# Half products for a third expert in the last three pairs, and for the fourth in the last pair

## The chip, the cores and the metric

The kernel runs on one core of a Trainium2 chip. The metric is the device time of one execution in microseconds, the median of several runs. The engines named below are TensorE (PE, with its weight loads shown apart as PEld), ScalarE (ACT), VectorE (DVE), GpSimd (POOL) and SyncE (SP, which issues DMAs). Each has a queue of its own; they meet through semaphores.

## The reference

Two stages follow each other. The first is attention over 4 batches, 8 heads, 768 positions and 64 values per head: heads 0, 2 and 6 see all earlier positions, the other five only the first 4 positions and a window of 64. Its output, laid out as 3072 tokens of 512 values, is the input x of the second stage, a mixture of 4 experts that are all evaluated for every token:

```python
N, D, E, F = (3072, 512, 4, 1024)
p = domain_probs / (domain_probs.sum(-1, keepdims=True) + 1e-09)
for e in range(E):
    h = np.maximum(x @ w1[e], 0.0)
    out += p[:, e:e + 1] * (h @ w2[e])
```

Since p is positive, it may be multiplied into x before the Relu; the kernel does so in the stretch that matters here.

## The kernel before

**Tiles and pairs.** The 3072 tokens are 24 tiles of 128. The first four tiles are done one way, while attention still supplies inputs. The other twenty are ten pairs of two tiles (256 tokens), in `pair_steps`. The change touches the last three of these pairs: the eighth (tiles 18 and 19), the ninth (20 and 21) and the tenth (22 and 23). By then attention is over; its buffers for keys (`kSf`), values (`vSf`, `kR`) and its PSUM banks `pV` are free for other use.

**Layer 1, plain.** `plain_layer1(e)` computes h = Relu(x w1) of one expert for 256 tokens. It is a generator with four steps. A step issues 8 matmuls of 256 columns (line 1199) into a PSUM bank from a pool of four (`pA`), then one Relu by ScalarE (line 1208).

**Layer 1 by half products.** `winograd_layer1(e, x, y)` computes the same with 7 products of half-size blocks instead of 8 (the scheme of Strassen in Winograd's form). It is a generator with seven steps. A step issues 8 matmuls of 128 columns (line 1228). Products 1, 3, 5 and 7 accumulate in bank x, 4 and 6 in bank y, product 2 goes to a bank of its own. ScalarE copies the partial sum out of the bank after products 1, 3 and 4 (line 1238). VectorE adds such a copy to a bank after products 2, 5 and 6 and applies the Relu (line 1245). ScalarE applies the Relu to bank x after product 7 (line 1278). A product may write a bank only after its last reader is done. The scheme needs sums of inputs (`scaled_sums`, lines 1166 and 992: three VectorE instructions, and one more after product 4) and sums of the weights (`first_weight_sums`, line 992: three into buffers, and a fourth that overwrites a block of w1), which are made once per expert.

**Which experts.** All pairs use half products for expert 3 (`EW[0]`). The last three (`two`) use them for expert 2 too (`EW[1]`), and the last two (`three`) for expert 1 (`EW3`), each with banks x and y: experts 3 and 1 share the two `pO` banks, expert 2 then has the two `pV` banks. Expert 0 is always plain.

**Order.** An order of steps is written out by hand for each kind of pair: a list of rows with the generators to advance and an operation to issue after them. `a`, `b` and `third` are the half products of experts 3, 2 and 1, and `n` a plain step. In the eighth pair it is (one step of `a`, `b` or `n` at a time): a a n a a n a a n n a b n b b n b b n b n b. In the ninth and tenth it is a b seven times, n, and then third third n three times, and third. So each engine's queue holds its work in exactly this order.

**Layer 2.** The same scheme is applied to h w2, over all four experts at once: 7 products of 16 matmuls of 256 columns (line 1361) in the two `pO` banks. The sums of blocks of h that it needs are made by VectorE: `first_sum` (line 1174) at the end of layer 1, second, third and fourth sums (line 992) during layer 2. During layer 2 VectorE also scales the next pair's inputs by the probabilities (`scale_inputs`, line 1150), which SP loads (`load_probs`, line 1127), and its outputs are stored by SP. Adds of layer 2 are on line 1384. The last pair ends with two shorter products (line 1453).

Of the kernel before, what the change touches and what calls it, by code (L numbers as in the profile page):

```python
# [19 lines left out]
def kernel(  # L20
# [42 lines left out]
    DMP = DM // P  # L63
# [50 lines left out]
    EW = (E - 1, E - 2)  # L114
    KH, FN = DMP // 2, F // 2
# [7 lines left out]
    kSf = pers.tile([P, NT * NSH * P], FP16, name="kS")  # L123
    vSf = pers.tile([P, NT * NSH * P], FP16, name="vS")
# [881 lines left out]
    t1 = {(EW[0], n): t1sb[:, n, :, :] for n in range(3)}  # L1006

    def first_weight_sums(e):

        return [  # L1010
            lambda: minus(t1[e, 0], w1_part(e, 0, 1), w1_part(e, 0, 0)),
            lambda: minus(t1[e, 1], w1_part(e, 1, 1), t1[e, 0]),
            lambda: minus(t1[e, 2], w1_part(e, 1, 0), t1[e, 1]),
            lambda: minus(w1_part(e, 0, 1), w1_part(e, 1, 1), w1_part(e, 0, 1)),
        ]
# [11 lines left out]
    EW3 = E - 3  # L1027

    def room_for_third():

        n = KH * FN
        for i in range(3):
            t1[EW3, i] = vSf[:, i * n : (i + 1) * n].rearrange("p (c f) -> p c f", c=KH)

    def inputs_for_third():
        n0 = 3 * KH * FN
        x = vSf[:, n0 : n0 + DMP * PC]
        own_room[EW3] = x.rearrange("p (c x) -> p c x", c=DMP)
# [72 lines left out]
    PC = PT * P  # L1111
# [10 lines left out]
    xs_of = [None]  # L1122

    def load_probs(nt0):
        pB_of[nt0] = moe.tile([P, PT, E, P], FP32, name="pB", tag="pB", bufs=1)
        rows = p_rows[nt0 : nt0 + PT, :]
        nc.sync.dma_start(
            out=pB_of[nt0].rearrange("p t e x -> p (t e x)"),
            in_=bass.AP(rows.tensor, rows.offset, [[0, P], [1, PT * E * P]]),
        )  # L1130
# [26 lines left out]
    second_set = set()  # L1157
# [6 lines left out]
    def scaled_sums(e):  # L1164

        nc.vector.tensor_tensor(
            out=x_sum(e, 0), in0=x_part(e, 1, 0), in1=x_part(e, 1, 1), op=ALU.add
        )
        minus(x_sum(e, 1), x_sum(e, 0), x_part(e, 0, 0))
        minus(x_part(e, 1, 0), x_part(e, 0, 0), x_part(e, 1, 0))  # L1170

    def first_sum(e, n=1):
        k = slice(e * HT, (e + n) * HT)
        nc.vector.tensor_tensor(
            out=S1[:, k, :], in0=A21[:, k, :], in1=A22[:, k, :], op=ALU.add
        )
# [9 lines left out]
        return nt0 >= pairs[-LAST]  # L1186

    def three(nt0):
        return nt0 >= pairs[-2]

    def pair_steps(nt0, nxt):

# [28 lines left out]
        def winograd_layer1(e, x, y, kept=kept):  # L1221

            ns = HT * KH * mm_ns(P)

            def product(ps, w, a, first):
                for f in range(HT):
                    for ct in range(KH):
                        nc.tensor.matmul(  # L1228
                            out=ps[:, f * P : (f + 1) * P],
                            lhsT=w_tile(e, w[:, ct, :], f),  # L1230
                            rhs=a[:, ct, :],
                            start=(first and f == 0 and ct == 0),
                            stop=(ct == KH - 1),
                            skip_group_check=True,
                        )

            def keep(n, ps):
                nc.scalar.copy(out=kept[n], in_=ps)  # L1238

            def block(n):  # L1240
                return blocks[:, n, e * HT : (e + 1) * HT, :]

            def add(n, ps, b):

                nc.vector._custom_dve(  # L1245
                    TENSOR_ADD_SAT,
                    out=block(b),
                    in0=ps.rearrange("p (f x) -> p f x", f=HT),
                    in1=kept[n].rearrange("p (f x) -> p f x", f=HT),
                    s0=LARGEST,  # L1250
                    s1=0.0,
                )

            def t(n):
                return t1[e, n]

            product(x, w1_part(e, 0, 0), x_part(e, 0, 0), True)
            keep(0, x)
            yield ns, 0.5
            z = bank()  # L1260
            product(z, w1_part(e, 1, 0), x_part(e, 0, 1), True)
            add(0, z, 0)
            yield ns, 0.5
            product(x, t(1), x_sum(e, 1), False)
            keep(1, x)
            yield ns, 0.5
            product(y, t(0), x_sum(e, 0), True)
            keep(2, y)
            minus(x_part(e, 0, 1), x_part(e, 0, 1), x_sum(e, 1))
            yield ns, 0.5  # L1270
            product(x, w1_part(e, 0, 1), x_part(e, 1, 0), False)
            add(2, x, 3)
            yield ns, 0.5
            product(y, w1_part(e, 1, 1), x_part(e, 0, 1), False)
            add(1, y, 2)
            yield ns, 0.5
            product(x, t(2), x_part(e, 1, 1), False)
            nc.scalar.activation(
                out=block(1), in_=x.rearrange("p (f x) -> p f x", f=HT), func=AF.Relu
            )  # L1280
            yield ns, 0.5
# [3 lines left out]
        a, b = (winograd_layer1(e, *y) for e, y in zip(EW, (banks, banks[::-1])))  # L1285
        if three(nt0):

            second_set.add(EW[1])
            more_kept = kSf[:, 0 : 4 * HT * P].bitcast(FP32)
            more_kept = [more_kept[:, n * HT * P : (n + 1) * HT * P] for n in (0, 1, 0)]  # L1290
            more_banks = [pV.tile([P, DM], FP32, name="pV", bufs=2) for _ in range(2)]
            b = winograd_layer1(EW[1], *more_banks, more_kept)
            third = winograd_layer1(EW3, *banks)

        more, last_more = [], None
        if nt0 == pairs[-LAST - 2]:
            room_for_more_sums()
            more = first_weight_sums(EW[1])
        elif nt0 == pairs[-LAST - 1]:
            last_more = first_weight_sums(EW[1])[3]  # L1300
        elif nt0 == pairs[-3]:
            room_for_third()
            more = first_weight_sums(EW3)
            last_more = more[3]
        if not two(nt0):
            n = itertools.chain(*(plain_layer1(e) for e in range(E - 1)))
            order = (
                ((n,), lambda: scale_inputs(nt0, 1)),
                ((n,), more[0] if more else None),
                ((n, a), lambda: last_weight_sum(E - 1) if nt0 == pair0 else None),  # L1310
                ((n, a), None),
                ((n, a), lambda: scale_inputs(nt0, 2)),
                ((n, a), lambda: load_probs(nxt)),
                ((n, a), more[1] if more else None),
                ((n, a), more[2] if more else None),
                ((n, a), lambda: first_sum(0, 2)),
                ((n,), None),
                ((n, n), lambda: first_sum(2, 2)),
                ((), lambda: scale_inputs(nxt, 1) if two(nxt) else None),
            )  # L1320
        elif three(nt0):
            n = plain_layer1(0)
            order = (
                ((), lambda: scaled_sums(EW[1])),
                ((a, b, a, b), lambda: load_probs(nxt) if nxt else None),
                ((a, b, a, b), None),
                ((a, b, a, b), None),
                ((a, b), lambda: scaled_sums(EW3)),
                ((n,), None),
                ((third, third, n), lambda: first_sum(EW[0])),  # L1330
                ((third, third, n), lambda: first_sum(EW[1])),
                ((third, third, n), lambda: first_sum(0)),
                ((third,), lambda: first_sum(EW3)),
            )
        else:
            n = itertools.chain(plain_layer1(0), plain_layer1(1))
            order = (
                ((a, a, n), more[0] if more else None),
                ((a, a, n), lambda: load_probs(nxt) if nxt else None),
                ((a, a, n), more[1] if more else None),  # L1340
                ((n,), lambda: scaled_sums(EW[1])),
                ((a, b, n), more[2] if more else None),
                ((b, b, n), lambda: first_sum(0)),
                ((b, b, n), lambda: first_sum(EW[0])),
                ((b, n, b), lambda: (first_sum(1), first_sum(EW[1]))),
            )
        for steps, op in order:
            for x in steps:
# [7 lines left out]
        x = pO.tile([P, DM], FP32, name="pO", bufs=2)[:, 0:HN]  # L1356
        y = pO.tile([P, DM], FP32, name="pO", bufs=2)[:, 0:HN]
# [47 lines left out]

        last = nxt is None
        ahead = nxt and two(nxt)
        if ahead and three(nxt):
            inputs_for_third()
        half = KT // 2 * mm_ns(HN), PSHARE  # L1410
        yield from product(x, A11, b(0, 0), True)
# [62 lines left out]
    pairs = list(range(pair0, NTILE, PT))  # L1474
# [145 lines left out]
```

The softmax here doesn't subtract the row's maximum and nothing guards it: scores larger than these inputs give would overflow.

## Time and profile before

| | us |
|---|---|
| median of 3 runs (lowest, highest) | 376.77 (376.42, 377.32) |
| the profiled execution | 376.68 |
| its span in the profile | 375.0 |
| TensorE busy in the span | 367.9 |
| layer 1 of the eighth pair | 13.24 (from 296.10 to 309.34) |
| layer 1 of the ninth pair | 12.88 (from 321.56 to 334.44) |
| layer 1 of the tenth pair | 13.01 (from 346.66 to 359.67) |

Times inside the profile are microseconds from the start of the span. In the timelines a row is one instruction, or several that follow each other: start, duration, engine, line, operation, the written tensor and what it is read from, shape and count. In brackets stands how long the engine had been idle and what ended that. The end of a matmul is modelled from its start, so the distance of two starts says how long the first occupied TensorE; a reader that waits for it can start only after the modelled end.

### The profile page before, as it was taken

What the parts mean: (1) busy time and instruction counts of PE and PEld (TensorE: products, weight loads), DVE (VectorE), ACT (ScalarE), POOL (GpSimd) and SP (SyncE); (2) the same over time, 40 slices, a digit from 0 to 9 for tenths busy, and PEclk for the clock granted to TensorE, in tenths of its full rate; (3) what the DMA queues carried; (4) which work ended last, traced back from release to release, by engine and by line L of the source; (5) the groups of instructions that cost most, each with busy time, mean ns of one, the idle gap of its engine ahead of it and who ended that gap; (6) DMA issues with size and microseconds to landing.
All of it is one profiled execution on the core that took longest, in us unless ns stands there. A gap on an engine that the chain in (4) does not pass through costs nothing.

```text
span 375.0 us, 10225 instructions
## 1 busy us (share of the span) xinstructions
PE 367.9 (98%) x4176; PEld 311.1 (83%) x4176; DVE 279.0 (74%) x599; ACT 227.4 (61%) x475; POOL 113.3 (30%) x155
## 2 busy tenths in 40 slices
PE   8899999999999999999999999999999999999996
PEld 5755466668998988999989898998899998998996
DVE  7774768697788669868658858957767968969762
ACT  3863478547785785765676955784778362450630
POOL 8924673982058038115601650320000000000000
PEclk9999999999999999999999999999999999999999
DMA  8999999999699569977904990951220300300101
GB/s 161 155 204 208 195 189 192 186 207 100 97 109 149 101 94 116 163 112 56 207 14 60 171 159 14 133 127 14 67 73 3 98 18 0 114 2 2 58 3 56
DMA packets 123747, 39.24 MB, mean 105 GB/s; under 512 B 113728, under 2 KB 116356, under 8 KB 123700
## 3 DMA queue, kind: packets, MB, share of 16 engines
q0 software_dynamic: 85824, 19.01, 58.7%
q1 hardware_dynamic: 36276, 19.18, 21.8%
q8 instruction: 32, 0.52, 0.6%
q10 hardware_dynamic: 1600, 0.39, 0.5%
q14 instruction: 15, 0.12, 0.1%
HBM read 44.89 MB, written 6.34 MB: 137 GB/s over the span
## 4 chain that ended last, share of the span: by engine, by line
PE 95%; DVE 2%; ACT 2%; issue 0%; ACTq 0%
PE pO L1361 31%; PE pA L1199 23%; PE pO L1228 9%; PE pA L1065 7%; PE pO L1086 7%; PE pA L678 5%; PE pV L734 2%; PE pV L806 2%; PE pA L1228 2%; PE pV L1228 1%; PE pO L448 1%; PE pA L576 1%; ACT es L696 1%; DVE xs L1150 1%; PE pA L1453 0%; ACT rc L824 0%
## 5 line engine op out<-in xcount | busy, mean ns | idle before, releaser
L1361 PEld LDWEIGHTS <-hA 128*128 128x128 f16 x1104 | 104.9, 98 | 12.3
L1199 PE MATMUL pA<-xs,w1sb 128*128 128x256 f16 x800 | 101.3, 273 | 0.0
L1199 PEld LDWEIGHTS <-w1sb 128*128 128x128 f16 x800 | 74.7, 98 | 7.9
L1208 ACT ACTIVATE hA<-pA 128x512 f16<-128x512 f32 x100 | 59.6, 598 | 31.2 <-PE pA L1199 29.0
L1361 PE MATMUL pO<-w2sb,hA 128*128 128x256 f16 x640 | 76.7, 272 | 0.0
L696 ACT ACTIVATE es<-pA 128x384 f16<-128x384 f32 (+2 forms) x122 | 59.2, 511 | 26.9 <-PE pA L678 23.0
L306 POOL DMA_DIRECT2D vS<-in_v_dram x30 | 29.6, 987 | 112.0 <-PE pV L806 111.0
L1361 PE MATMUL pO<-tsb,hA 128*128 128x256 f16 x464 | 56.7, 272 | 0.0
L1150 DVE TENSOR_TENSOR xs<-xT,pB 128x1024 f16<-128x1024 f16 (+1 forms) x49 | 47.0, 977 | 0.0
L992 DVE TENSOR_TENSOR hA<-hA 128x1024 f16<-128x1024 f16 x60 | 39.5, 685 | 0.5
L1078 ACT ACTIVATE hA<-pA 128x384 f16<-128x384 f32 (+1 forms) x64 | 22.2, 385 | 19.4 <-PE pA L1065 19.2
L1065 PE MATMUL pA<-xT,w1sb 128*128 128x384 f16 (+1 forms) x256 | 30.9, 273 | 0.8 <-DMA w1sb<-in_moe_w_dram 0.5
L1086 PE MATMUL pO<-w2sb,hA 128*128 128x512 f16 x128 | 30.7, 379 | 0.0
L1228 PEld LDWEIGHTS <-w1sb 128*128 128x128 f16 x480 | 29.6, 98 | 1.2 <-issue 0.2
L829 DVE TENSOR_TENSOR xT<-pV,rc 64x384 f16<-64x384 f32 x37 | 20.5, 554 | 11.8 <-ACT rc L834 9.4
L1381 ACT COPY s<-pO 128x256 f32<-128x256 f32 x31 | 11.5, 373 | 27.7 <-PE pO L1361 21.9
L1065 PEld LDWEIGHTS <-w1sb 128*128 128x128 f16 x256 | 19.4, 98 | 9.7 <-issue 1.4
L824 ACT ACTIVATE rc<-pV,eps 64x384 f32<-64x384 f32 x37 | 21.3, 576 | 6.5 <-PE pV L806 5.9
L700 DVE TENSOR_TENSOR es<-es,mS 128x384 f16<-128x384 f16 (+1 forms) x40 | 13.7, 344 | 15.0 <-ACT es L696 15.0
L1245 DVE CUSTOM_DVE_ANT_0 hA<-pO,s 128x512 f16<-128x512 f32 x26 | 17.6, 688 | 9.7 <-PE pO L1228 8.3
L1238 ACT COPY s<-pO 128x512 f32<-128x512 f32 x39 | 22.5, 587 | 2.3 <-PE pO L1228 2.0
L678 PE MATMUL pA<-qT,kR 128*128 128x384 f16 (+2 forms) x120 | 22.9, 278 | 0.4 <-DVE kR L595 0.2
(163 smaller groups left out, 515.6 us busy)
## 6 DMA issues: line engine op xcount, KB each, us to landing
pB<-p_rows SPq DMA_DIRECT2D x10, 512.0 KB
out_dram<-o SPq DMA_DIRECT2D x19, 256.0 KB
w1sb<-in_moe_w_dram POOLq DMA_DIRECT2D x8, 512.0 KB, 9.1
w2sb<-in_moe_w_dram POOLq DMA_DIRECT2D x4, 1024.0 KB, 12.4
vS<-in_v_dram POOLq DMA_DIRECT2D x30, 112.0 KB, 4.3
k_rows<-in_k_dram POOLq DMA_DIRECT2D x18, 128.0 KB, 5.5
q<-in_q_dram POOLq DMA_DIRECT2D x18, 128.0 KB, 7.0
vR<-in_v_dram POOLq DMA_DIRECT2D x24, 48.0 KB, 5.8
```

Source lines behind the costliest of these rows:

```text
L306: gp.dma_start(out=t[:, :, own_v(h)], in_=windows_of(v, b, h, c))
L678: nc.tensor.matmul(out=ps[:, o : o + nq], lhsT=key_tile(b, c, h, t), rhs=qTs[b, c][:, hp, q0 : q0 + nq], start=(n == 0 or not first), stop ...
L696: nc.scalar.activation(out=es[:, 0:cols], in_=ps[:, 0:cols], func=AF.Exp, scale=SC)
L992: nc.vector.tensor_tensor(out=out, in0=a, in1=b, op=ALU.subtract)
L1065: nc.tensor.matmul(out=pss[ft][:, 0:cols_n], lhsT=w1_tile(e, ct, ft), rhs=x[:, ct, :], start=(n == 0), stop=(n == DMP - 1),)
L1086: nc.tensor.matmul(out=ps_o, lhsT=hs[:, ft, j * P : (j + 1) * P], rhs=w2sb[:, e * FTP + ft, :], start=(ft == 0), stop=(ft == FTP - 1),)
L1150: nc.vector.tensor_tensor(out=o, in0=xin, in1=pb.to_broadcast([P, DMP, n, P]), op=ALU.mult)
L1199: nc.tensor.matmul(out=ps[:, f * PC : (f + 1) * PC], lhsT=w1_tile(e, ct, f0 + f), rhs=xs[:, ct, :], start=(ct == 0), stop=(ct == DMP - 1),)
L1208: nc.scalar.activation(out=blocks[:, b0 : b0 + 2, k0 : k0 + 2, :].rearrange("p t f x -> p f t x"), in_=ps.rearrange("p (f t x) -> p f t x" ...
L1228: nc.tensor.matmul(out=ps[:, f * P : (f + 1) * P], lhsT=w_tile(e, w[:, ct, :], f), rhs=a[:, ct, :], start=(first and f == 0 and ct == 0), ...
L1238: nc.scalar.copy(out=kept[n], in_=ps)
L1361: nc.tensor.matmul(out=ps, lhsT=a[:, k, :], rhs=b(k), start=(first and k == 0), stop=(k == KT - 1), skip_group_check=not first,)
```

## The change

The eighth pair gets the half products for expert 1 that the ninth and tenth have, and the tenth pair gets them for expert 0 too. Expert 0's products (`fourth`) use the banks of expert 2 after it. Room for its three weight sums is found in the buffers of values, keys and scaled inputs.

The weight sums of expert 1, made during the eighth pair for the ninth, are now needed within the eighth, so they are issued earlier relative to its products; those of expert 0 are made in the ninth pair. The fourth weight sum of expert 1, issued at the end of layer 2 of the eighth pair before, moves into its layer 1; the fourth of expert 0 comes at the end of the ninth pair.

The ninth pair keeps its products, with the weight sums and first sums at other rows. The eighth pair's new order is: a a n b b n a b a b a b a b n a b third third n third third third third third. The tenth pair's is a b seven times, and then third fourth seven times.

```diff
+    def room_for_fourth():
+        n = KH * FN
+        x = [vSf[:, 4 * n : 5 * n], kSf[:, 2560 : 2560 + n]]
+        x.append(xs_of[0][:, DMP * PC : 2 * DMP * PC])
+        for i, y in enumerate(x):
+            t1[0, i] = y.rearrange("p (c f) -> p c f", c=KH)
...
     def three(nt0):
-        return nt0 >= pairs[-2]
+        return nt0 >= pairs[-3]
...
             third = winograd_layer1(EW3, *banks)
+            if nxt is None:
+                second_set.add(0)
+                fourth = winograd_layer1(0, *more_banks, more_kept)
...
             more = first_weight_sums(EW3)
+        elif nt0 == pairs[-2]:
+            room_for_fourth()
+            more = first_weight_sums(0)
             last_more = more[3]
...
+        elif nxt is None:
+            order = (
+                ((), lambda: scaled_sums(EW[1])),
+                ((a, b, a, b), None),
+                ((a, b, a, b), lambda: scaled_sums(EW3)),
+                ((a, b, a, b, a, b), lambda: scaled_sums(0)),
+                ((third, fourth, third, fourth), lambda: first_sum(EW[0])),
+                ((third, fourth, third, fourth), lambda: first_sum(EW[1])),
+                ((third, fourth, third, fourth), None),
+                ((third, fourth), lambda: (first_sum(EW3), first_sum(0))),
+            )
+        elif nt0 == pairs[-3]:
+            n = plain_layer1(0)
+            order = (
+                ((a, a, n), lambda: scaled_sums(EW[1])),
+                ((b, b, n), more[0]),
+                ((a, b, a, b), more[1]),
+                ((a, b, a, b), more[2]),
+                ((n, a, b), lambda: (scaled_sums(EW3), load_probs(nxt))),
+                ((third, third, n), more[3]),
+                ((third, third), lambda: first_sum(EW[0])),
+                ((third, third), lambda: first_sum(EW[1])),
+                ((third,), lambda: (first_sum(0), first_sum(EW3))),
+            )
         elif three(nt0):
...
-                ((n,), None),
+                ((n,), more[0]),
                 ((third, third, n), lambda: first_sum(EW[0])),
-                ((third, third, n), lambda: first_sum(EW[1])),
-                ((third, third, n), lambda: first_sum(0)),
-                ((third,), lambda: first_sum(EW3)),
-            )
-        else:
-            n = itertools.chain(plain_layer1(0), plain_layer1(1))
-            order = (
-                ((a, a, n), more[0] if more else None),
-                ((a, a, n), lambda: load_probs(nxt) if nxt else None),
-                ((a, a, n), more[1] if more else None),
-                ((n,), lambda: scaled_sums(EW[1])),
-                ((a, b, n), more[2] if more else None),
-                ((b, b, n), lambda: first_sum(0)),
-                ((b, b, n), lambda: first_sum(EW[0])),
-                ((b, n, b), lambda: (first_sum(1), first_sum(EW[1]))),
-            )
+                ((third, third, n), more[1]),
+                ((third, third, n), lambda: (first_sum(EW[1]), first_sum(0))),
+                ((third,), lambda: (first_sum(EW3), more[2]())),
+            )
...
-        if ahead and three(nxt):
+        if ahead and three(nt0):
             inputs_for_third()
```

More of the change, by code (lines that the diff above doesn't have):

```diff
@@ L1324, in pair_steps @@
                 ((), lambda: scaled_sums(EW[1])),
-                ((a, b, a, b), lambda: load_probs(nxt) if nxt else None),
+                ((a, b, a, b), lambda: load_probs(nxt)),
                 ((a, b, a, b), None),
```

## The prediction

> **What bounds the kernel now.** I read the page's busy times first, then the chain that ended last, then the layer-1 stretches of the last three pairs, and last the engines' timelines there. On the page:
>
> ```profile
> PE 367.9 (98%) x4176; PEld 311.1 (83%) x4176; DVE 279.0 (74%) x599; ACT 227.4 (61%) x475; POOL 113.3 (30%) x155
> ...
> PE 95%; DVE 2%; ACT 2%; issue 0%; ACTq 0%
> ```
>
> TensorE is busy 98% of the span and carries 95% of the chain, so a saved matmul or a new wait on TensorE counts in full. Busy time by engine over layer 1 of the eighth, ninth and tenth pair (the stretches between the layers' first matmuls):
>
> ```profile
> 296.10:309.34 13.24, 13.24 (x178) 12.51 (x177) 9.21 (x18) 8.38 (x16) 0.00 (x0) 1.00 0.28 82
> 321.56:334.44 12.88, 12.88 (x203) 12.51 (x201) 9.60 (x23) 8.08 (x16) 0.00 (x0) 1.00 0.25 83
> 346.66:359.67 13.01, 13.01 (x203) 12.55 (x200) 9.04 (x21) 8.13 (x16) 0.00 (x0) 1.00 0.11 42
> ```
>
> Columns: length, PE, PEld, DVE, ACT, POOL, granted clock, DMA. PE fills each stretch at full clock; DVE has 3 to 4 us free. TensorE's timeline (start, duration to the modelled end):
>
> ```profile
> 326.92 0.61 PE L1228 MATMUL pO<-xs,t1sb 128*128 128x128 f16 x8
> 327.37 0.61 PE L1228 MATMUL pV<-xs,t 128*128 128x128 f16 x8
> 327.82 1.04 PE L1199 MATMUL pA<-xs,w1sb 128*128 128x256 f16 x8
> 328.69 0.61 PE L1228 MATMUL pO<-vS,w1sb 128*128 128x128 f16 x8
> ...
> 346.66 0.61 PE L1228 MATMUL pO<-xs,w1sb 128*128 128x128 f16 x8
> 347.25 0.61 PE L1228 MATMUL pV<-xs,w1sb 128*128 128x128 f16 x8
> ```
>
> Starts give the prices. A product of the half scheme (8 matmuls of 128 columns) takes 327.37 - 326.92 = 0.447 us, a plain step (8 of 256 columns) 328.69 - 327.82 = 0.873 us. The last two rows are the only gap: 0.59 instead of 0.447, so 0.14 us.
>
> The readers of those PSUM banks, from ScalarE's and VectorE's timelines:
>
> ```profile
> 327.57 0.60 ACT L1278 ACTIVATE hA<-pO 128x512 f16<-128x512 f32 x1 [1.52 <-PE pO L1228]
> 328.06 0.59 ACT L1278 ACTIVATE hA<-pV 128x512 f16<-128x512 f32 x1
> ...
> 325.89 0.69 DVE L1245 CUSTOM_DVE_ANT_0 hA<-pO,s 128x512 f16<-128x512 f32 x1 [0.72 <-PE pO L1228]
> 326.50 0.68 DVE L1245 CUSTOM_DVE_ANT_0 hA<-pV,kS 128x512 f16<-128x512 f32 x1
> ...
> 345.98 1.21 DVE L1150 TENSOR_TENSOR xs<-xT,pB 128x1024 f16<-128x1024 f16 x1
> ```
>
> The Relu starts 0.04 after its product's modelled end (326.92 + 0.61 = 327.53) and takes 0.60. The add starts 0.14 after its product's (325.14 + 0.61 = 325.75), takes 0.69, and a second follows 0.60 later. The scaling ends at 347.19 and the matmul held by it starts at 347.25: 0.06 to restart. So a bank is free for the next product this long after its product's start: **1.30 us when ScalarE reads it** (0.61 + 0.04 + 0.59 + 0.06), **1.49 us when VectorE does** (0.61 + 0.14 + 0.68 + 0.06). Two products are 0.89 us, four are 1.79, two and a plain step 1.77. In the kernel before, the next product on such a bank comes at least 1.77 us after the last (C5 at 332.22, C7 at 333.99, in the letters below); that is why PE shows no such gap.
>
> **What the Trainium skill says.** "TensorE: Matmul & The Clock Gate", section "Wait — 56ns, not 53.3ns?", gives 55.8 ns between warm 128-column matmuls; the trace agrees (0.447 / 8 = 55.9). Its section "Back-to-back issue gap" gives about 81 ns for sustained pairs of weight load and matmul; the trace contradicts that, and the trace decides. Its section "Step-by-step: what each phase is for" says that matmuls stay in program order and only weight loads are pulled ahead, so one matmul waiting for a bank holds all behind it; the gap at 347.25 fits. "PSUM — Partial Sum Buffer", section "Engine vs sequencer instructions", says that ScalarE's and VectorE's queues are strictly first in, first out, so an add behind another add frees its bank later.
>
> **The change, part by part.** Write A, B, C, D for experts 3, 2, 1, 0, and A5 for A's fifth product. Each expert's products use bank x in 1, 3, 5, 7 and bank y in 4, 6. Copies by ScalarE read 1, 3 and 4; adds by VectorE read 5 (x) and 6 (y); ScalarE's Relu reads 7 (x). Product 2 has a bank of its own. A and C share banks, B and D another two.
>
> *Saving.* In the eighth pair C goes from plain to half products, in the tenth D does. Each drops 4 x 0.873 = 3.494 and adds 7 x 0.447 = 3.128: -0.366 each, -0.73 together. The ninth pair's TensorE order stays.
>
> *Eighth pair, new waits.* The order is A1 A2 D B1 B2 D A3 B3 A4 B4 A5 B5 A6 B6 D A7 B7 C1 C2 D C3 C4 C5 C6 C7, then layer 2: one expert's worth of plain steps is gone, and C's end stands bare.
> - C1 writes bank x two products after A7: 1.30 - 0.89 = 0.41; A7's Relu starts 0.05 later since D's Relu stands before it (they follow 0.49 apart): 0.45.
> - C5 two products after C3, again with D's Relu ahead of the copy: 0.45.
> - C6 waits for the copy of C4, which follows C3's by 0.48: 0.04.
> - C7 needs the add of C5: 1.49 - 0.89, less the 0.04 just spent: 0.56.
> - Layer 2's first product takes bank y (in the trace of before it starts 0.447 after C7, before C7's Relu has run, so it is not on x). The add of C6 follows that of C5 by 0.60: C5 + 0.75 + 0.60 + 0.69 + 0.06 = 2.10 after C5, where C7 ends 1.49 + 0.45 = 1.94 after it: 0.15.
>
> Sum 1.65, net +1.28. All stand on the path; what is queued behind is layer 2, and for that every engine waits. VectorE's other work here (three weight sums, the scaled sums, C's adds, the last weight sum moved from layer 2) stands in gaps: by its rows C's scaled sums end near 305.9 and are first needed after 307. The first sums end 1.2 us into layer 2, before 1.4 (S2's start now).
>
> *Ninth pair.* VectorE gets three weight sums of D (0.60 each): two stand where it idled 0.91 and 1.40 us, the third before S2, which slips to +1.8 and is needed at +3.5. Nothing. Without that cover it would be 0.6 each.
>
> *Tenth pair.* A and B interleave as before. VectorE has one more weight sum (0.60) before B's scaled sums, as the ninth pair has today without a gap; C's scaled sums (0.73) fall into the 0.72 it idles before the add of A5. Then A7 B7 C1 D1: C1 two products after A7: 0.41. D1: B7's Relu starts 0.49 after A7's: 0.04. C and D interleave, four products apart: 1.79 covers both releases. D7 clears by about 0.1, and layer 2's first product waits 0.02 for the add of C6, behind D5's. Sum 0.47, net +0.10. The 0.14 gap at its start stays.
>
> *DMAs and other queues.* Layer 2, GpSimd's and SP's orders stay. The load of probabilities for the ninth pair is issued later in program order, but is SP's next item with the same wait and not needed before layer 2: nothing.
>
> **Sum.** -0.73 + 1.65 + 0.47 = +1.39. The profiled execution took 376.68 with 375.0 of span; the span becomes 376.4 and the time 378.07; on the median of 376.77 it is 378.16. I say **378.1**.
>
> What the trace does not show is a matmul held by a bank's reader. Bounds for eight such waits: each could end up to 0.15 earlier (release when the next instruction of the reader may start, 0.49 or 0.60, and no restart cost), or 0.08 later (a restart twice as dear). I take the 0.06 seen at 347.25. Ends: +0.6 and +1.9, so 377.3 and 378.7.
>
> **Rivals.**
> 1. *Readers release early.* At the first of those bounds C1, C5 and the tenth pair's C1 cost some 0.3 each, C7 0.4, the rest nothing: 1.3 less 0.73 is +0.6, 377.3, no difference to be told. For it: rows on ScalarE follow 0.49 apart though each lasts 0.60. Against: the scaling at 345.98 would by its spacing of 1.13 have let the matmul go at 347.11 with no gap at all, and there is a gap. It decides once the waits sum to under 1.48.
> 2. *The saving stands alone:* all waits hidden, 376.0. For it: no product waits for a bank today. Against: every product of today has more than 1.49 us to its bank's reader, and the new order leaves 0.89. Dearer products are not to be expected: all of today's run at 55.9 ns a matmul.
> 3. *VectorE becomes the bound in the tenth pair.* Its layer 1 needs 12 adds x 0.60 + 3 x 0.73 of scaled sums + 4 x 0.20 + 4 x 0.34 of first sums + 0.60 + the scaling's last 0.5 = 12.7 us against 13.1 available. With margins of 0.1 at D7 and none at layer 2, each slip counts at once; half a microsecond gives 378.6, and the first sums behind it would make S2 late only after 1 us more.
>
> **How the numbers follow.** A measurement can tell some 0.2%, 0.75 us, from no change: below 376.02 is faster, above 377.52 slower. The forecast has 0.76 (its own range 377.6 to 378.6), VectorE's bound 0.08, early release 0.12, the saving alone 0.04. Slower: 0.76 + 0.08, less 0.01 for the edge; same 0.13; faster 0.04. The range reaches from the early release (377.3) to a little above the late bound, 378.8; under 2 in 10 is left out.
>
> **What would show it.** In the changed profile: layer 1 of the eighth pair about 14.5 us long (13.24 now), with gaps before C1, C5, C7 and layer 2 of 0.45, 0.45, 0.56 and 0.15; the ninth 12.88; the tenth about 13.1, with one gap of 0.4 before C1. The chain should show ScalarE and VectorE links there. I am wrong if the eighth pair's C1 to C7 run 0.447 apart, if layer 2's first product waits for C7's Relu (0.7 more), or if the ninth pair shows gaps.

## The result and the profile after

The changed kernel takes 377.95 us (median of 10 runs, 377.87 to 378.47), against 376.82 us of the kernel before (median of 10 runs, 376.42 to 377.65). The ratio is 1.003, with a 95% interval of 1.0019 to 1.004: the change costs about 1.1 us. The forecast was 378.1. All executions behind these figures and those below had a granted clock of 0.999 or 1.00, save the profiled one of the first run with an exchanged bank (0.853, 424.47 us), which no ratio contains.

On the page of the changed kernel TensorE has 48 matmuls more (4224 for 4176) and is busy about as long as before (367.7 us for 367.9). VectorE is busy 7.9 us longer.

```profile
span 376.7 us, 10349 instructions
...
PE 367.7 (98%) x4224; PEld 310.9 (83%) x4224; DVE 286.9 (76%) x617; ACT 227.4 (60%) x475; POOL 113.3 (30%) x155
```

Busy time by engine in layer 1 of the eighth, ninth and tenth pair of the changed kernel (length, then PE, PEld, DVE, ACT, POOL, granted clock, DMA share and rate):

```profile
296.52:311.02 14.50, 13.56 (x202) 12.75 (x201) 12.23 (x26) 8.32 (x16) 0.00 (x0) 1.00 0.23 75
323.24:336.11 12.87, 12.87 (x202) 12.51 (x200) 10.21 (x24) 8.09 (x16) 0.00 (x0) 1.00 0.23 83
348.34:361.43 13.09, 12.85 (x226) 12.63 (x224) 11.69 (x29) 8.03 (x16) 0.00 (x0) 1.00 0.12 43
```

Before, these were 13.24, 12.88 and 13.01. The eighth pair has become 1.26 us longer, the ninth is the same, and the tenth is 0.08 longer: 1.33 together. In the first and the last TensorE no longer fills the stretch. Its busy time hides part of each wait, since a matmul counts as busy to its modelled end: the eighth pair's 13.56 us are for products that take 12.87 us where none of them waits (the spread order below). Who kept it waiting in the changed kernel from the eighth pair on stands in the list of waits (total, times, longest):

```profile
PE pO L1236 <- ACT hA L1286: 0.5, 2, 0.3
PE pO L1236 <- DVE hA L1253: 0.4, 1, 0.4
PE pO L1236 <- ACT s L1246: 0.3, 1, 0.3
```

Lines 1236, 1286, 1246 and 1253 are the half products, ScalarE's Relu after product 7, its copy, and VectorE's add: the readers of the banks. TensorE's timeline of the changed kernel at the end of the eighth pair's layer 1 shows each place. As in the prediction, A, B, C and D stand for experts 3, 2, 1 and 0, and A7 for A's seventh product. The rows are A7, B7, C1, C2, a plain step of D, C3 with C4, C5 with C6, C7, and layer 2:

```profile
304.50 0.61 PE L1236 MATMUL pO<-xs,t1sb 128*128 128x128 f16 x8
304.95 0.61 PE L1236 MATMUL pV<-xs,t 128*128 128x128 f16 x8
305.84 0.61 PE L1236 MATMUL pO<-xs,w1sb 128*128 128x128 f16 x8 [0.28 <-ACT hA L1286]
306.28 0.61 PE L1236 MATMUL pA<-xs,w1sb 128*128 128x128 f16 x8
306.73 1.04 PE L1207 MATMUL pA<-xs,w1sb 128*128 128x256 f16 x8
307.60 1.06 PE L1236 MATMUL pO<-kS,vS 128*128 128x128 f16 x16
308.93 1.10 PE L1236 MATMUL pO<-xs,w1sb 128*128 128x128 f16 x16 [0.27 <-ACT s L1246]
310.42 0.61 PE L1236 MATMUL pO<-xs,vS 128*128 128x128 f16 x8 [0.39 <-DVE hA L1253]
311.02 0.27 PE L1387 MATMUL pO<-w2sb,hA 128*128 128x256 f16 x1
```

The loss has to be read from start to start. The brackets give only the time after the modelled end of the work ahead, and that end lies 0.16 us (0.61 - 0.447) behind the moment when TensorE could have taken the next matmul. From B7 to C1 it is 305.84 - 304.95 = 0.89 where 0.447 was needed: 0.44 lost, with 0.28 in the bracket. In the same way C5 lost 308.93 - 307.60 - 0.89 = 0.44, C6 and C7 together 310.42 - 308.93 - 0.89 = 0.60, and layer 2 0.15. The readers stand in ScalarE's and VectorE's timelines of the changed kernel:

```profile
305.20 0.59 ACT L1286 ACTIVATE hA<-pO 128x512 f16<-128x512 f32 x1
...
308.30 1.07 ACT L1246 COPY s<-pO 128x512 f32<-128x512 f32 x2
```

```profile
307.77 0.68 DVE L992 TENSOR_TENSOR w1sb<-w1sb 128x1024 f16<-128x1024 f16 x1
...
309.68 1.29 DVE L1253 CUSTOM_DVE_ANT_0 hA<-pO,s 128x512 f16<-128x512 f32 x2 [0.69 <-PE pO L1236]
```

A7's Relu ends at 305.79, and C1 goes at 305.84. The two copies of C3 and C4 end at 309.37, and C6 goes at 309.42, within the row that starts at 308.93 (308.93 + 1.10 - 0.61). The two adds of C5 and C6 end at 310.97, and layer 2 goes at 311.02. Each time TensorE starts 0.05 us after the reader's end.

Late data does not explain these starts. C5 reads the fourth weight sum of expert 1, which is the first VectorE row above: it ends at 308.45, 0.48 before C5 goes. The last sum of inputs, which C6 reads, ends at 308.65, and the third weight sum, which C7 reads, at 305.67. Layer 2's first product reads only the first block of h, whose last writer, the add of C2, ends at 307.85.

In the tenth pair A7, B7, C1 and D1 follow each other as:

```profile
353.83 0.61 PE L1236 MATMUL pO<-xs,t1sb 128*128 128x128 f16 x8
354.28 0.61 PE L1236 MATMUL pV<-xs,t 128*128 128x128 f16 x8
355.13 0.61 PE L1236 MATMUL pO<-vS,w1sb 128*128 128x128 f16 x8 [0.24 <-ACT hA L1286]
355.62 0.61 PE L1236 MATMUL pV<-xs,w1sb 128*128 128x128 f16 x8
```

C1 loses 355.13 - 354.28 - 0.447 = 0.40, and D1 loses 0.04. C1 comes 1.30 us after A7, the price that was worked out for a bank that ScalarE reads.

The chain of work that ended last, in the changed kernel, now passes through ScalarE and VectorE at the end of the eighth pair (start, duration, what):

```profile
305.20 0.60 ACT hA L1286
...
309.68 0.70 DVE hA L1253
```

The span grew by 1.7 us, 0.4 more than these stretches. That part lies ahead of the eighth pair, which starts at 296.52 instead of 296.10 although every instruction up to there is the same: the waits listed for TensorE in the first 60 us come to 4.4 us instead of 3.6. In the profiles of the kernels below, whose instructions up to there are also the same, the eighth pair starts between 295.75 and 296.43, so this is scatter of single executions and no effect of the change. The profiled execution, 378.47 us, was the slowest of its ten. The medians, with 1.13 us between them, are the better measure of the whole, and the stretches of its parts.

### The profile page after: what moved, and what is told of

Same layout as the page of the kernel before. It is cut to its first block, busy times and chain, and to the rows that moved or that the text cites. A ratio compares the mean times of both kernels' runs of the same rounds, so it can differ in the third digit from the quotient of the medians.

```text
span 376.7 us, 10349 instructions
## 1 busy us (share of the span) xinstructions
PE 367.7 (98%) x4224; PEld 310.9 (83%) x4224; DVE 286.9 (76%) x617; ACT 227.4 (60%) x475; POOL 113.3 (30%) x155
## 4 chain that ended last, share of the span: by engine, by line
PE 86%; DMA 7%; POOL 3%; DVE 1%; ACT 1%; issue 1%; POOLq 0%; ACTq 0%; DVEq 0%
PE pO L1387 31%; PE pA L1207 21%; PE pO L1236 9%; DMA w2sb<-in_moe_w_dram 7%; PE pO L1094 6%; PE pA L678 5%; PE pA L1073 5%; PE pV L1236 3%; PE pA L1236 2%; PE pV L734 2%; PE pV L806 2%; POOL vS L310 1%; POOL vR L304 1%; DVE xs L1158 1%; PE pA L1479 0%
## 5 line engine op out<-in xcount | busy, mean ns | idle before, releaser
L1207 PE MATMUL pA<-xs,w1sb 128*128 128x256 f16 x736 | 93.2, 272 | 0.0
L1207 PEld LDWEIGHTS <-w1sb 128*128 128x128 f16 x736 | 68.7, 98 | 7.3
L1216 ACT ACTIVATE hA<-pA 128x512 f16<-128x512 f32 x92 | 54.9, 599 | 28.5 <-PE pA L1207 26.4
L1236 PEld LDWEIGHTS <-w1sb 128*128 128x128 f16 x544 | 33.2, 98 | 2.2 <-issue 1.3
L1073 PEld LDWEIGHTS <-w1sb 128*128 128x128 f16 x256 | 19.3, 98 | 9.8 <-issue 1.8
```

Source lines behind the costliest of these rows:

```text
L1073: nc.tensor.matmul(out=pss[ft][:, 0:cols_n], lhsT=w1_tile(e, ct, ft), rhs=x[:, ct, :], start=(n == 0), stop=(n == DMP - 1),)
L1207: nc.tensor.matmul(out=ps[:, f * PC : (f + 1) * PC], lhsT=w1_tile(e, ct, f0 + f), rhs=xs[:, ct, :], start=(ct == 0), stop=(ct == DMP - 1),)
L1216: nc.scalar.activation(out=blocks[:, b0 : b0 + 2, k0 : k0 + 2, :].rearrange("p t f x -> p f t x"), in_=ps.rearrange("p (f t x) -> p f t x" ...
L1236: nc.tensor.matmul(out=ps[:, f * P : (f + 1) * P], lhsT=w_tile(e, w[:, ct, :], f), rhs=a[:, ct, :], start=(first and f == 0 and ct == 0), ...
```

## The experiments

**The theory:** a product that writes a PSUM bank must come 1.30 us (bank read by ScalarE) or 1.49 us (read by VectorE) after the start of the last product there, and the new order leaves 0.89 in five places of the eighth pair's end and at C1 and D1 of the tenth; this is the whole loss, and the products save what was counted. **The rival:** the loss is VectorE's added work (sums of inputs and weights, adds), which holds TensorE whatever the order. Each ratio below is to the kernel before, run alongside.

**The eighth pair alone undone.** It gets its old order and products back; the tenth keeps the change.

```diff
-        if three(nt0):
+        if nt0 >= pairs[-2]:
             second_set.add(EW[1])
...
             room_for_third()
             more = first_weight_sums(EW3)
+            last_more = more[3]
...
         elif nt0 == pairs[-3]:
-            n = plain_layer1(0)
+            n = itertools.chain(plain_layer1(0), plain_layer1(1))
             order = (
...
```

> The eighth pair's layer 1 as in the kernel before (experts 3 and 2 by half products), the tenth as in the changed kernel. Bank theory (a product waits 1.30 us after the last one on its bank where ScalarE reads it, 1.49 where VectorE does): the eighth pair's layer 1 is back at 13.24 us without a gap, the tenth stays 13.1 with one gap of 0.40 before C1; time 376.82 + 0.08 = 376.9, the same as before. Rival (VectorE is overloaded, and the tenth pair with its 12.7 us of VectorE work is where the time goes): most of the loss stays, 377.5 or more.

Measured: 376.89 us, ratio 0.9999 (0.9989 to 1.0009). Layer 1 of the three pairs takes 13.24, 12.88 and 13.11 us. The loss is gone, so it is the eighth pair's. The tenth pair's own balance is about +0.1, too small for the times to tell and seen in the stretch alone; in this run it lies in three places, 0.06 before B7, 0.34 before C1 and 0.06 before D1.

**The tenth pair alone undone.** The ninth and tenth get their old operations back (no `fourth`, none of its weight sums; the first sums stay at their new rows); the eighth keeps the change.

```diff
-            if nxt is None:
-                second_set.add(0)
-                fourth = winograd_layer1(0, *more_banks, more_kept)
...
-        elif nxt is None:
-            order = (
...
```

> The ninth and tenth pair as in the kernel before (no half products for expert 0, none of its weight sums), the eighth as in the changed kernel. Bank theory: the eighth's layer 1 stays 14.5 us with gaps of 0.44, 0.44, 0.56 and 0.15; the tenth is back at 13.0; time 377.95 - 0.08 = 377.9. Rival (VectorE overloaded in the tenth): the loss goes, 376.5 to 376.9.

Measured: 377.92 us, ratio 1.0031 (1.0021 to 1.004). Layer 1 takes 14.49, 12.87 and 13.01 us. All of the loss is still there, without expert 0's half products and their VectorE work.

**One bank exchanged.** Nothing but C's two banks in the eighth pair changes places.

```diff
-            third = winograd_layer1(EW3, *banks)
+            third = winograd_layer1(EW3, *(banks[::-1] if nt0 == pairs[-3] else banks))
```

> The changed kernel with one edit: in the eighth pair C's banks x and y are exchanged, the order of all instructions stays. C1 then writes the bank that the add of A6 frees early, not the one that A7's Relu reads. Bank theory: the gap of 0.44 before C1 is gone, those before C5 (0.36 to 0.44), C7 (0.56) and layer 2 stay or layer 2's grows to 0.8 if its first product is then on the bank of C7's Relu; layer 1 is 14.1 us, time 377.5 (or 14.7 and 378.2). Rival (C1 waits for data or for the weight load, not the bank): the gap stays 0.44, layer 1 14.5, time 377.95.

Measured: 377.48 us, ratio 1.0016 (1.0007 to 1.0026). The same kernel was run once more for its profile:

> The kernel with C's banks exchanged in the eighth pair once more, for its profile. Bank theory: no gap before C1; before C5, C7 and layer 2 gaps of 0.36 to 0.44, 0.56 and 0.15, layer 1 14.1 us (its time of 377.48 speaks for this). Rival: a gap of 0.44 before C1.

Measured: 377.72 us, ratio 1.0018 (1.0007 to 1.0028). The timeline of TensorE of that run, from A7 on (rows as above):

```profile
304.17 0.61 PE L1236 MATMUL pO<-xs,t1sb 128*128 128x128 f16 x8
304.61 0.61 PE L1236 MATMUL pV<-xs,t 128*128 128x128 f16 x8
305.06 0.61 PE L1236 MATMUL pO<-xs,w1sb 128*128 128x128 f16 x8
305.51 0.61 PE L1236 MATMUL pA<-xs,w1sb 128*128 128x128 f16 x8
...
308.15 1.10 PE L1236 MATMUL pO<-xs,w1sb 128*128 128x128 f16 x16 [0.27 <-ACT s L1246]
309.64 0.60 PE L1236 MATMUL pO<-xs,vS 128*128 128x128 f16 x8 [0.39 <-DVE hA L1253]
310.24 1.47 PE L1387 MATMUL pO<-w2sb,hA 128*128 128x256 f16 x12
```

C1 now follows B7 after 0.45: its gap is gone, with every instruction in its old place and C1's data no earlier. So C1 waited for the bank and not for data or for weights. The other gaps stay, and layer 1 is 14.05 us. Layer 2's wait stays 0.15 although C7 now stands on the other bank, so layer 2's first product does not wait for C7's Relu here either.

**One plain step moved.** A step of D goes from between B2 and A3 to between C4 and C5.

```diff
-                ((b, b, n), more[0]),
+                ((b, b), more[0]),
...
-                ((third, third), lambda: first_sum(EW[0])),
+                ((third, third, n), lambda: first_sum(EW[0])),
                 ((third, third), lambda: first_sum(EW[1])),
```

> The changed kernel with one plain step of expert 0 in the eighth pair moved from between B2 and A3 to between C4 and C5. Bank theory: the gap before C5 (0.44) and that before C6 (0.04) go, those before C1 (0.44), C7 (0.60) and layer 2 (0.15) stay; layer 1 is 14.05 us, time 377.5. Rival (VectorE late with the sums): C5 then waits as before, or the gap moves to C6 or C7, layer 1 14.5 and time 377.95.

Measured: 377.61 us, ratio 1.002 (1.001 to 1.003), layer 1 14.06 us. In the timeline of TensorE of this run, C3 with C4, the moved step, C5 with C6, C7 and layer 2 follow as:

```profile
305.96 1.06 PE L1236 MATMUL pO<-kS,vS 128*128 128x128 f16 x16
306.85 1.04 PE L1207 MATMUL pA<-xs,w1sb 128*128 128x256 f16 x8
307.72 1.06 PE L1236 MATMUL pO<-xs,w1sb 128*128 128x128 f16 x16
309.22 0.61 PE L1236 MATMUL pO<-xs,vS 128*128 128x128 f16 x8 [0.44 <-DVE hA L1253]
309.81 1.91 PE L1387 MATMUL pO<-w2sb,hA 128*128 128x256 f16 x16
```

The gap before C5 is gone and nothing replaces it. C7 still waits 0.61 for the add of C5, since C5 to C7 is still bare. Here the gap went where the step was put, and the others stayed. By itself this would also fit a C5 that waits for late data, since C5 now comes later; the times of its data given above speak against that.

**All of the eighth pair spread.** The same products in an order that leaves each bank its time: after A2, C2, C4 and C6 stands a plain step each, C's banks are exchanged so that C1 follows A6's bank, and two weight sums come later.

```diff
-            third = winograd_layer1(EW3, *banks)
+            third = winograd_layer1(EW3, *(banks[::-1] if nt0 == pairs[-3] else banks))
...
-                ((b, b, n), more[0]),
-                ((a, b, a, b), more[1]),
-                ((a, b, a, b), more[2]),
-                ((n, a, b), lambda: (scaled_sums(EW3), load_probs(nxt))),
+                ((b, b), more[0]),
+                ((a, b, a, b), None),
+                ((a, b, a, b), more[1]),
+                ((a, b), lambda: (scaled_sums(EW3), load_probs(nxt))),
                 ((third, third, n), more[3]),
-                ((third, third), lambda: first_sum(EW[0])),
-                ((third, third), lambda: first_sum(EW[1])),
-                ((third,), lambda: (first_sum(0), first_sum(EW3))),
+                ((third, third, n), lambda: (first_sum(EW[0]), more[2]())),
+                ((third, third, n), lambda: (first_sum(EW[1]), first_sum(0))),
+                ((third,), lambda: first_sum(EW3)),
```

> The changed kernel with the eighth pair's same products in another order: plain steps of expert 0 after A2, C2, C4 and C6, and the banks x and y of C exchanged, so that C1 takes the bank that the add of A6 frees. Two weight sums of C are issued later. Bank theory: each product on a bank comes at least 1.77 us after the last (C1: 1.79 after A6); the eighth's layer 1 is 12.9 us without gaps of 0.1 or more; time 377.95 - 1.6 = 376.35. Rival (the extra VectorE sums within the eighth pair hold TensorE): the number of VectorE instructions is the same, so layer 1 stays above 14 us and the time above 377.5.

Measured: 376.32 us, ratio 0.9988 (0.9981 to 0.9996). Layer 1 takes 12.87, 12.87 and 13.09 us. VectorE has as many instructions as in the changed kernel (617), and TensorE does not wait in the eighth pair. In this run's layer 1 of the eighth pair, VectorE is busy for 12.25 of 12.87 us, nearly full, and still holds nothing up:

```profile
295.87:308.74 12.87, 12.87 (x200) 12.44 (x200) 12.25 (x26) 8.06 (x16) 0.00 (x0) 1.00 0.25 85
```

One distance is shorter than the 1.77 us that was expected at least: B3 follows B1 after 1.34 us (297.63 to 298.97). That is enough: where C1 and C5 had to wait behind a Relu of D, they went 1.34 and 1.33 us after the product ahead on their bank. The run changes three things at once; the exchanged bank and a moved plain step have runs of their own, the later weight sums have none.

**The tenth pair reordered as well.** On top of the spread order, C and D exchange their banks in the tenth pair and begin C1 C2 D1 D2, so that C1 comes 1.79 us after A6 and D1 2.24 us after B6.

```diff
-            third = winograd_layer1(EW3, *(banks[::-1] if nt0 == pairs[-3] else banks))
+            third = winograd_layer1(EW3, *(banks if nt0 == pairs[-2] else banks[::-1]))
...
-                fourth = winograd_layer1(0, *more_banks, more_kept)
+                fourth = winograd_layer1(0, *more_banks[::-1], more_kept)
...
-                ((third, fourth, third, fourth), lambda: first_sum(EW[0])),
+                ((third, third, fourth, fourth), lambda: first_sum(EW[0])),
```

> As the run with the spread order in the eighth pair, and in the tenth the banks x and y of C and D exchanged and the first four of their products ordered C1 C2 D1 D2. Bank theory: the tenth's layer 1 falls from 13.09 to 12.7 us, its gap of 0.40 before C1 gone, 0.14 at its start left; time 376.35 - 0.39 = 375.95, so 0.2% faster than before, all of the saving of 0.73 but some 0.05. Rival (VectorE's 12.7 us of work there are the bound): the gap comes back elsewhere in the tenth pair, 13.0 us or more, 376.3.

Measured: 375.95 us, ratio 0.9979 (0.9969 to 0.999). Layer 1 takes 12.87, 12.87 and 12.65 us. This beats both kernels: by the ratios some 1.9 us under the changed one, and 0.7 us under the one before that was run alongside (376.65). It is the saving that the products had promised. Busy time in the tenth pair of this run:

```profile
346.23:358.88 12.65, 12.65 (x226) 12.55 (x224) 11.78 (x29) 8.01 (x16) 0.00 (x0) 1.00 0.12 45
```

**The last gap.** On top of that, the scaling of B's inputs in the tenth pair is split by tiles, as the ninth pair has it.

```diff
-        for g, c0, t0, n in pieces(nt0):
+        parts = list(pieces(nt0))
+        if e == EW[1] and nt0 == pairs[-1]:
+            parts = [(g, c0 + i * P, t0 + i, 1) for g, c0, t0, n in parts for i in range(n)]
+        for g, c0, t0, n in parts:
```

> The kernel with both pairs reordered, and in the tenth pair the scaling of B's inputs (1.21 us, whose end B1 waits for) split into one instruction for each tile of tokens, as the ninth pair has it already; B1 needs the first tile alone. Theory: the gap of 0.14 before B1 goes, the tenth pair's layer 1 is 12.55 us, time 375.95 - 0.14 = 375.8. Rival: the added VectorE time (0.07) in the pair with the least VectorE room moves the gap to layer 2 or to C1, no gain.

Measured: 376.03 us, ratio 0.9971 (0.9957 to 0.9985). The tenth pair's layer 1 is 12.53 us, and B1 follows A1 after 0.45 in its timeline:

```profile
346.46 0.61 PE L1239 MATMUL pO<-xs,w1sb 128*128 128x128 f16 x8
346.91 0.61 PE L1239 MATMUL pV<-xs,w1sb 128*128 128x128 f16 x8
```

So the gap is gone from the stretch (0.12 us), but the times cannot tell this kernel from the last one: the median is not lower, and the intervals of the ratios overlap. The expected 375.8 us was not reached.

## Why the prediction was right

- **The saving** of 0.366 for each expert, -0.73: shown by the reordered kernel, whose eighth pair is 0.37 shorter than before (12.87 for 13.24) and whose tenth is 0.36 shorter (12.65 for 13.01).
- **The eighth pair's waits:** 0.45, 0.45, 0.04, 0.56 and 0.15 were worked out; 0.44, 0.44, 0.60 for C6 and C7 together, and 0.15 were measured. The net of +1.28 came out as +1.26. That the wait is for the bank is shown for C1 by the exchanged bank (and for the tenth pair's C1, which follows B7 without a gap once its bank is exchanged). For C5, C6, C7 and layer 2 it rests on the timeline, where each goes 0.05 after the bank's reader, with its data ready earlier; the moved step (C5, C6) and the spread order (all four) agree. Layer 2's place on the bank of C6 is right: its first product went before C7's Relu had run.
- **The ninth pair** was to stay the same, with S2 slipping to 1.8 us into layer 2: 12.87 us, and VectorE's second sums start at 337.93, 1.82 after layer 2.
- **The tenth pair:** 0.41 and 0.04 for C1 and D1, and 0.02 at layer 2, were worked out; the starts give 0.40 and 0.04, and nothing at layer 2. The net of +0.10 came out as +0.08.
- **The sum** of +1.39 is +1.33 in the stretches and +1.13 in the medians (0.7 to 1.5 by the interval). The restart of 0.06, the one cost for which the profile before had a single example, was 0.05. The upper end of the range was worked out loosely: eight waits longer by 0.08 add 0.64 and give +2.0, not +1.9, and a restart twice as dear is 0.06 more. The measured time lies below the forecast, so this end was not tried.
- **The rivals:** readers that release early fall, since C1 would then have lost 0.3. The saving alone came true only where the order was changed. VectorE as the bound of the tenth pair falls too: in the reordered kernel it is busy 11.78 us of that pair's 12.65, and the one gap that it causes is the 0.14 at the start, which stood there before the change. The 12.7 us that the rival counted hold some 0.7 of first sums that run after layer 1.

## What to carry to other kernels

Before products are cut into smaller ones, count for each PSUM bank the time from one product's start to the next on the same bank, and compare it with the product's latency, the reader's start, its duration and the restart (in this kernel 1.30 us by ScalarE and 1.49 us by VectorE for 128 x 512 fp32). A scheme with fewer, shorter products saves TensorE's time only while other work fills these distances: the same products cost 1.1 us in one order and gave 0.7 us in another, with some banks exchanged. When a plain stretch of work is replaced, ask what it covered besides its own result.

## What the runs showed of the hardware

- The idle time that a timeline puts in brackets before a matmul understates the loss, by the 0.16 us by which the modelled end of the matmul ahead exceeds its issue: 0.28 for 0.44 before C1, 0.27 for 0.44 before C5.
- VectorE at 93 to 95% busy (11.78 of 12.65 us, 12.25 of 12.87) did not slow TensorE where the order left each bank its time, apart from the 0.14 at the start of the tenth pair.
- A product that waited for its bank came 1.30 us after the product ahead on it where ScalarE read the bank (353.83 to 355.13), and 1.49 us where VectorE did (308.93 to 310.42). It started 0.05 us after the reader's end.
